# A decode attention layer on one core: whole-tile VectorE steps, a re-tiled query projection, and a wo block in small transfers

## The chip, the core and the metric

The kernel runs on one core of a Trainium2 chip. The core has a matrix engine (TensorE, "PE"; its weight loads are "PEld"), VectorE ("DVE"), ScalarE ("ACT"), GpSimd ("POOL") and SyncE ("SP"), which here only issues transfers. Sixteen DMA engines move data from the device memory into the on-chip memory of 128 partitions. Each engine runs its own list of instructions in order; engines wait for each other on semaphores.

The metric is the device time of one execution in microseconds. Before the change it is 664.11 us, the median of three runs (664.04 to 664.16).

## The reference, cut to what matters

Four requests, one new token each. The token's vector of 640 numbers is normalised; from it a query projection gives 32 heads of 128 numbers, and each head attends over its own cache of 4096 keys and values. The result goes through `wo`. A small gated MLP on the same normalised vector and the token itself are added.

```python
x = A_x                                   # (4, 1, 640)
xn = _layernorm(x)
q = (xn @ wq).reshape(B, 1, 32, 128).transpose(0, 2, 1, 3)
scores = jnp.einsum('bhqd,bhkd->bhqk', q, k_cache) * 128 ** -0.5    # k_cache (4, 32, 4096, 128)
p = softmax(scores)
o = jnp.einsum('bhqk,bhkd->bhqd', p, v_cache)
A = o.transpose(0, 2, 1, 3).reshape(B, 1, 4096) @ wo                # wo (4096, 640)
out = x + A + gated_mlp(xn, w_in, w_sp, b_sp, w_out)
```

Everything is bfloat16. The caches are 2 x 134 MB and each element is used once, so nearly all bytes that are read are keys and values.

## The kernel before

**Tiles and slots.** The 32 heads are cut into 8 groups (`HG`) of 4 heads (`HT`). A tile is one group of one request: 4 heads x 4096 positions x 128, 4 MB, laid over 128 partitions so that partition 32h + l holds 128 consecutive positions (`NC` "columns" of 128 numbers) of head h; the 32 partitions of a head are its "lanes" (`LN`). There are 32 tiles of keys and 32 of values; tile i is group i // 4, request i % 4. All of them pass through five slots of 4 MB (`KV_SLOTS`), which at the start hold the two parts of `wq` and the MLP's weights.

**Loads.** All large loads are issued by SyncE. `loads` (L128) is the order: keys 0 and 1, then values i and keys i + 2 in turn, with one more key tile ahead before tiles 24 and 28 (`EXTRA_K`). `pump` (L140) issues the next loads whose slots are marked as used; SyncE then waits until the engines have really finished with the slot. The last values are cut in four. The blocks of `wo` (640 KB, one for each group) are loaded by `load_wo` (L153): blocks 0 to 6 at the end of the third tile of their group (L698), block 7 at the end in four parts (L157).

**Start.** x is normalised and transposed to `xnT`. The query projection (L267 to L276) has the weights of `wq` as the stationary operand, 128 x 128 for each of 32 heads and 5 slices of the 640 inputs, and 4 columns of `xnT` moving: 160 matmuls; the result, `qT`, has the head's 128 numbers along the partitions. `stage_q` (L421) makes of it, tile by tile, a query for each of the 128 lanes: a transpose once a group, then one matmul with `q_lanes`, copied to `qbc` by ScalarE. `gmlp` computes the MLP. GpSimd prepares constants.

**The loop over tiles** (L662 to L699) is written out by hand: inside `manual_schedule` TensorE, VectorE, ScalarE and SyncE keep the order of the code. For tile i:

- Keys: VectorE multiplies the tile in place by the query (`product`, L441), folds 128 numbers to 64 by one addition (`fold_half`, L450), TensorE adds the 64 in steps of 8 through the identity (`sums`, L459, eight matmuls of 512 columns), and VectorE sums the last 8 (`row_sums`, L470). All of this is done in two halves of 64 columns, `product(i, 0)`, `fold_half(i, 0)`, `sums(i, 0)`, then the same for half 1; `row_sums(i, 1)` comes in tile i + 1, after `product(i + 1, 0)`.
- Softmax of tile i - 1, spread over tile i: the lanes' maximum (`lane_max`, L479, VectorE), laid out by ScalarE (L485), spread to the head by a matmul (L492), the head's maximum `nb` (`head_max`, L499, VectorE, after the first fold of tile i), the exponentials (`exps`, L508, ScalarE), and the mask on GpSimd (L517), which lays p out for the value matmuls as `pm`.
- Values of tile j = i - 1 (i - 2 and i - 3 after the extra key tiles): `blocks` (L532), 32 matmuls on 32 columns each, four side by side; for odd j a copy (L542) and `gather` (L553).
- At a group's last tile: denominators (`group_den`, L577 to L586: GpSimd, TensorE, VectorE's reciprocal), `group_norm` (L591), `group_turn`, and one tile later `group_pick` and `group_proj` (L631), eight matmuls of the group's result with its `wo` block into `out_ps`.

On TensorE the order in a tile is therefore: spread of the maximum, `sums` of half 0, the query, the value blocks of tile j, gather, `sums` of half 1. On VectorE it is: product 0, row sums 1 of the last tile, lane maximum, fold 0, head maximum, product 1, (reciprocal), row sums 0, fold 1, (group norm).

**End.** After the loop come the softmax of tile 31, the last two value tiles, the group's norm, `group_proj` of group 7, copies of `out_ps` and the transfers of the output.

Of the kernel before, what the change touches and what calls it, by code (L numbers as in the profile page):

```python
# [15 lines left out]
KV_SLOTS = 5  # L16
EXTRA_K = (24, 28)
ALIGN = 512


@with_exitstack
def kernel(
# [130 lines left out]
    def load_wo(j):  # L153
        wo_tiles[j] = wop.tile([P, HT, D], BF16, name="wo")
        if j == HG - 1:
            for hh in range(HT):
                nc.sync.dma_start(out=wo_tiles[j][:, hh, :], in_=wo_h[j][:, hh, :])  # L157
            return
        nc.sync.dma_start(out=wo_tiles[j][:].rearrange("p r n -> p (r n)"), in_=wo_r[j])

    pump()

# [100 lines left out]
    xnT = const.tile([P, DC, Bsz], BF16)  # L263
    nc.vector.tensor_copy(out=xnT[:], in_=xnT_ps[:])

    q_ps = ps_m.tile([P, H, Bsz], FP32, tag="m", name="q_ps")
    for h in range(H):  # L267
        for c in range(DC):
            t, i = wq_parts[c]
# [38 lines left out]
    def gmlp():  # L308
        zz, gw, gt, gz, sq = (gm[n] for n in ("zz", "gw", "gt", "gz", "sq"))
        zT = ps_pv.tile([P, 2, NFC, Bsz], FP32, tag="pv", name="zT")  # L310
        for t in range(2):
            f1 = t * Fh + NFF * P
            w_t = w_in_sb[:, :, t * Fh : f1].rearrange("p c (f k) -> p c k f", k=NFF)
            for k in range(NFC):
                for c in range(DC):
                    nc.tensor.matmul(
                        out=zT[: P if k < NFF else FT, t, k, :],
                        lhsT=w_t[:, c, k, :] if k < NFF else w_in_sb[:, c, f1 : f1 + FT],
                        rhs=xnT[:, c, :],
                        start=(c == 0),  # L320
                        stop=(c == DC - 1),
                    )
# [93 lines left out]
    qbcs, scores, pvs, blocks_sb = {}, {}, {}, {}  # L416
    sums_ps, maxes = {}, {}

    q_rows = {}

    def stage_q(i):  # L421
        hg, b = divmod(i, Bsz)
        if b == 0:
            qr_ps = ps_m.tile([HT * Bsz, Dh], BF16, tag="m", name="qr_ps")
            nc.tensor.transpose(
                out=qr_ps[:],
                in_=qT[:, HT * hg : HT * (hg + 1), :].rearrange("p h b -> p (h b)"),
                identity=ident[:],
            )
            q_rows[hg] = small.tile([HT * Bsz, Dh], BF16, name="q_rows")  # L430
            nc.scalar.copy(out=q_rows[hg][:], in_=qr_ps[:])  # L431
        qb_ps = ps_m.tile([P, Dh], FP32, tag="m", name="qbc_ps")
        nc.tensor.matmul(  # L433
            out=qb_ps[:], lhsT=q_lanes[:, b, :], rhs=q_rows[hg][:], start=True, stop=True
        )
        qbcs[i] = small.tile([P, Dh], BF16, name="qbc", bufs=3)
        nc.scalar.copy(out=qbcs[i][:], in_=qb_ps[:])  # L437

    def product(i, half):
        t = k_tiles[i][:, half * HC : (half + 1) * HC, :]  # L440
        nc.vector.tensor_tensor(  # L441
            out=t,
            in0=t,
            in1=qbcs[i][:, None, :].to_broadcast([P, HC, Dh]),
            op=ALU.mult,
        )

    def fold_half(i, half):
        t = k_tiles[i][:, half * HC : (half + 1) * HC, :]
        nc.vector.tensor_tensor(  # L450
            out=t[:, :, 0:HD2], in0=t[:, :, 0:HD2], in1=t[:, :, HD2:Dh], op=ALU.add
        )

    def sums(i, half):
        t = k_tiles[i][:, half * HC : (half + 1) * HC, :]
        s = sums_ps[i, half] = ps_s.tile([P, HC, RW], FP32, name="s_ps")
        n = HD2 // RW
        for g in range(n):
            nc.tensor.matmul(  # L459
                out=s[:],  # L460
                lhsT=ident[:],
                rhs=t[:, :, g * RW : (g + 1) * RW],
                start=(g == 0),
                stop=(g == n - 1),
            )

    def row_sums(i, half):
        if half == 0:
            scores[i] = small.tile([P, NC], FP32, name="s_sb")
        nc.vector.tensor_reduce(  # L470
            out=scores[i][:, half * HC : (half + 1) * HC],
            in_=sums_ps.pop((i, half))[:],
            axis=AX.X,
            op=ALU.add,
        )

    def lane_max(i):
# [165 lines left out]
    def at(i, fn, *args):  # L643
        if 0 <= i < NT:
            fn(i, *args)
# [9 lines left out]
    E = mybir.EngineType  # L655
    with tc.manual_schedule(engines={E.PE, E.DVE, E.Activation, E.SP}):
        stage_q(0)
        stage_q(1)
# [94 lines left out]
```

## Time and profile before

| | |
|---|---|
| median of 3 runs | 664.11 us (664.04 to 664.16) |
| the profiled execution: its time / its span | 664.67 us / 662.8 us |
| busy: TensorE, VectorE, ScalarE, GpSimd | 52%, 74%, 8%, 23% of the span |
| read from device memory | 282.24 MB, 426 GB/s over the span |
| products (L441): number, mean | 64, 4.42 us |
| folds (L450): number, mean | 64, 2.37 us |
| GpSimd masks (L517): number, mean | 32, 4.45 us |
| VectorE idle before products, waiting for keys | 100.2 us |

The profile is of one execution; times in it are microseconds from the start of the span. A line of a group reads: source line, engine, operation, tile written <- tiles read, shape, number; in a timeline the two numbers in front are start and duration, and in brackets stands how long the engine was idle before and what ended that. In the chain of waits each row is start, duration and what the time went to; "DMA x<-y" is a transfer from its issue to its landing. An engine's name with a q (SPq) is its sequencer, which issues transfers. In the list of DMA queues q1 is SyncE's, q10 ScalarE's, and q8 and q14 read program code; the columns are packets, MB and share of the sixteen engines' time.

### The profile page before, as it was taken

How to read it: one execution, taken by the hardware profiler on the slowest of the kernel's cores; microseconds unless marked ns; L12 is line 12 of the kernel's file. 1: busy time of each engine (PE TensorE's matmuls, PEld its weight loads, DVE VectorE, ACT ScalarE, POOL GpSimd, SP SyncE). 2: the span in 40 equal slices, each digit the busy share in tenths (PEclk: the TensorE clock that was granted, in tenths of full speed). 3: DMA queues.
4: the chain of work that ended last, by engine and by line, in shares of the span. 5: the costliest groups of instructions: out<-in, count | busy, mean ns of one | idle time of the engine just before them, and what ended most of it. 6: DMA issues, size and time to landing. Idle time of an engine off the chain costs nothing.

```text
span 662.8 us, 5338 instructions
## 1 busy us (share of the span) xinstructions
PE 344.5 (52%) x2205; PEld 144.1 (22%) x2205; DVE 492.9 (74%) x334; ACT 52.5 (8%) x161; POOL 150.2 (23%) x51
## 2 busy tenths in 40 slices
PE   0636553636646545653437644474654655434576
PEld 0512221212222121221212212131211212212133
DVE  3289797867789677788767698767787899776960
ACT  0201100000010000100000001000100000000010
POOL 2002222112222112222112222112222132222220
PEclk9998676777576677776776657758666767678676
DMA  8999999999999999999999999999999999999996
GB/s 368 430 438 423 434 439 432 431 437 422 436 429 436 437 424 437 432 430 437 431 429 437 424 439 435 428 439 428 431 439 427 432 436 426 439 424 437 437 422 262
DMA packets 11972, 282.59 MB, mean 426 GB/s; under 512 B 1344, under 2 KB 1964, under 8 KB 3244
## 3 DMA queue, kind: packets, MB, share of 16 engines
q1 hardware_dynamic: 11928, 282.25, 99.0%
q8 instruction: 17, 0.28, 0.2%
q14 instruction: 7, 0.06, 0.0%
q10 hardware_dynamic: 20, 0.01, 0.0%
HBM read 282.24 MB, written 0.01 MB: 426 GB/s over the span
## 4 chain that ended last, share of the span: by engine, by line
issue 44%; DMA 29%; POOL 14%; DVE 9%; PE 3%; SPq 0%; ACT 0%; POOLq 0%; DVEq 0%; ACTq 0%
DMA k_nat<-in_A_k_cache_dram 21%; POOL pm L517 14%; DMA v_nat<-in_A_v_cache_dram 6%; DVE k_nat L441 5%; DVE k_nat L450 3%; PE s_ps L459 2%; DMA wo<-in_A_wo_dram 2%; PE pv_acc L532 1%; DVE s_sb L470 1%; DVE m L479 0%; PE pv L553 0%; POOL own_sum L577 0%; SPq L92 0%; SPq L104 0%; ACT pv_sb L542 0%
## 5 line engine op out<-in xcount | busy, mean ns | idle before, releaser
L441 DVE TENSOR_TENSOR k_nat<-k_nat,qbc 128x8192 bf16<-128x8192 bf16 x64 | 282.9, 4420 | 100.4 <-DMA k_nat<-in_A_k_cache_dram 100.2
L517 POOL TENSOR_TENSOR pm<-p,hmask_bf 128x512 bf16<-128x512 bf16 x32 | 142.4, 4452 | 496.2 <-ACT p L508 496.2
L459 PE MATMUL s_ps<-k_nat,ident 128*128 128x512 bf16 x512 | 188.9, 535 | 67.0 <-DVE k_nat L450 67.0
L450 DVE TENSOR_TENSOR k_nat<-k_nat 128x4096 bf16<-128x4096 bf16 x64 | 151.9, 2373 | 0.0
L492 PE MATMUL max_ps<-lay,head_scale 128*128 128x32 f32 x64 | 19.0, 388 | 176.3 <-ACT lay L485 176.3
L532 PE MATMUL pv_acc<-v_nat,pm 128*32 128x512 bf16 x1008 | 85.0, 498 | 39.0 <-POOL pm L517 35.6
L459 PEld LDWEIGHTS <-ident 128*128 128x128 bf16 x512 | 67.6, 134 | 168.6 <-issue 151.1
L492 PEld LDWEIGHTS max_ps<-lay,head_scale 128*128 128x128 f32 x64 | 14.8, 288 | 190.5 <-ACT lay L485 190.5
L532 PEld LDWEIGHTS <-pm 128*32 128x32 bf16 x1008 | 29.5, 117 | 82.4 <-POOL pm L517 42.1
L470 DVE TENSOR_REDUCE s_sb<-s_ps 128x64 f32<-128x512 f32 x64 | 43.4, 677 | 4.1 <-PE s_ps L459 4.1
L485 ACT ACTIVATE lay<-lane_diag,m 128x32 f32<-128x32 f32 x32 | 10.3, 321 | 340.2 <-DVE m L479 340.2
L586 DVE RECIPROCAL rden<-den 128x16 f32<-128x16 f32 x8 | 2.1, 258 | 30.5 <-PE den L584 30.5
L553 PE MATMUL pv<-sel,pv_sb 128*128 128x8 f32 x128 | 18.6, 272 | 9.3 <-ACT pv_sb L542 9.3
L553 PEld LDWEIGHTS pv<-sel,pv_sb 128*128 128x128 f32 x128 | 17.1, 208 | 15.8 <-ACT pv_sb L542 15.8
L508 ACT ACTIVATE p<-s_sb,nb 128x128 bf16<-128x128 f32 x32 | 12.8, 401 | 63.8 <-DVE nb L499 63.8
L437 ACT CAST qbc<-qbc_ps 128x128 bf16<-128x128 f32 x32 | 8.4, 267 | 85.1 <-PE qbc_ps L433 85.1
L542 ACT COPY pv_sb<-pv_acc 128x512 f32<-128x512 f32 x16 | 9.4, 586 | 65.6 <-PE pv_acc L532 65.6
L479 DVE TENSOR_REDUCE m<-s_sb 128x1 f32<-128x128 f32 x32 | 9.2, 286 | 1.1
L433 PE MATMUL qbc_ps<-q_rows,q_lanes 16*128 16x128 bf16 x32 | 8.2, 264 | 2.7 <-ACT q_rows L431 2.7
L278 DVE CAST qT<-q_ps 128x128 bf16<-128x128 f32 x1 | 0.3, 292 | 12.5 <-PE q_ps L270 12.5
L270 PE MATMUL q_ps<-xnT,wq 128*128 128x4 bf16 x160 | 4.6, 166 | 8.7 <-DMA wq<-in_A_wq_dram 8.7
L631 PE MATMUL out_ps<-wo,o_r 128*4 128x320 bf16 x56 | 8.0, 435 | 0.0
(90 smaller groups left out, 89.7 us busy)
## 6 DMA issues: line engine op xcount, KB each, us to landing
k_nat<-in_A_k_cache_dram SPq DMA_DIRECT2D x32, 4096.0 KB, 38.7
v_nat<-in_A_v_cache_dram SPq DMA_DIRECT2D x31, 4096.0 KB, 33.3
wo<-in_A_wo_dram SPq DMA_DIRECT2D x7, 640.0 KB, 40.5
wq<-in_A_wq_dram SPq DMA_DIRECT2D x1, 4096.0 KB, 12.7
w_sb<-in_B_w_in_dram SPq DMA_DIRECT2D x1, 2160.0 KB, 19.4
v_nat<-in_A_v_cache_dram SPq DMA_DIRECT2D x1, 2048.0 KB
wq<-in_A_wq_dram SPq DMA_DIRECT2D x1, 1024.0 KB, 14.7
v_nat<-in_A_v_cache_dram SPq DMA_DIRECT2D x1, 1024.0 KB
```

What stands on the lines that cost most here:

```text
L441: nc.vector.tensor_tensor(out=t, in0=t, in1=qbcs[i][:, None, :].to_broadcast([P, HC, Dh]), op=ALU.mult,)
L450: nc.vector.tensor_tensor(out=t[:, :, 0:HD2], in0=t[:, :, 0:HD2], in1=t[:, :, HD2:Dh], op=ALU.add)
L459: nc.tensor.matmul(out=s[:], lhsT=ident[:], rhs=t[:, :, g * RW : (g + 1) * RW], start=(g == 0), stop=(g == n - 1),)
L470: nc.vector.tensor_reduce(out=scores[i][:, half * HC : (half + 1) * HC], in_=sums_ps.pop((i, half))[:], axis=AX.X, op=ALU.add,)
L479: nc.vector.tensor_reduce(out=m1[:], in_=scores[i][:], axis=AX.X, op=ALU.max)
L485: nc.scalar.activation(out=d[:], in_=lane_diag[:], func=ACT.Copy, scale=maxes[i][:, 0:1])
L492: nc.tensor.matmul(out=ps[:], lhsT=head_scale[:], rhs=maxes[i][:], start=True, stop=True)
L508: nc.scalar.activation(out=p[:], in_=scores.pop(i)[:], func=ACT.Exp, bias=nb[:], scale=scale_qk, accum_out=acc[hg % NACC][:, b : b + 1],)
L517: nc.gpsimd.tensor_tensor(out=p_m[b][:, :, e : e + GC * HT].rearrange("p g (c h) -> p g c h", h=HT), in0=p[:].rearrange("p (g c) -> p g c" ...
L532: nc.tensor.matmul(out=pv_acc[g * LN : (g + 1) * LN, :], lhsT=pm[:, c // GC, :], rhs=v_nat[:, c : c + GC, :].rearrange("p c d -> p (c d)") ...
L542: nc.scalar.copy(out=pv_sb[:], in_=pv_acc[:])
L553: nc.tensor.matmul(out=pvs[hg][:, :, b - 1 : b + 1], lhsT=pv_sb[:, k * Dh : (k + 1) * Dh], rhs=sel[:, k, :, :], start=(k == 0), stop=stop ...
```

## The change

- **VectorE's steps are a whole tile each.** `product(i)`, `fold(i)` and `row_sums(i)` work on 128 columns at once; `sums(i)` is 16 matmuls into one buffer of two banks (`ps_s` has one buffer instead of two). The order in a tile becomes, on VectorE: product, row sums of the last tile, lane maximum, fold, head maximum, (reciprocal, group norm); on TensorE: spread of the maximum, (queries of the next group), value blocks of tile j, gather, all of `sums(i)`.
- **The query projection** has `xnT` (padded with zeros to 32 columns) as the stationary operand and 512 columns of `wq` moving: 5 slices x 8 groups, 40 matmuls, each group on its own 32 output partitions. VectorE and ScalarE copy one half of the result each. `stage_q` now works a group at a time: four matmuls with a new constant `place` gather the group's heads, then four with `q_lanes` make the queries of all four requests; it is called once before the loop and in the third tile of each group.
- **wo block 6** is loaded after the loop, ahead of block 7, and `group_proj(6)` is called just before `group_proj(7)`. The pool of `wo` tiles has two buffers.
- **wo block 0** is loaded in nine transfers: eight of 8 partitions each, then one of the other 64.

```diff
+WO_PARTS = (*range(0, 65, 8), 128)
...
-    wop = ctx.enter_context(tc.tile_pool(name="wop", bufs=1))
+    wop = ctx.enter_context(tc.tile_pool(name="wop", bufs=2))
...
-    ps_s = ctx.enter_context(tc.tile_pool(name="ps_s", bufs=2, space=PSUM))
+    ps_s = ctx.enter_context(tc.tile_pool(name="ps_s", bufs=1, space=PSUM))
...
-        nc.sync.dma_start(out=wo_tiles[j][:].rearrange("p r n -> p (r n)"), in_=wo_r[j])
+        rows = wo_tiles[j][:].rearrange("p r n -> p (r n)")
+        parts = WO_PARTS if j == 0 else (0, P)
+        for p0, p1 in zip(parts, parts[1:]):
+            nc.sync.dma_start(out=rows[p0:p1], in_=wo_r[j][p0:p1])
...
+    place = const.tile([P, HT, HT * Bsz], BF16)
+    nc.gpsimd.memset(place[:], 0.0)
+    for hh in range(HT):
+        nc.gpsimd.tensor_copy(
+            out=place[:, hh, hh * Bsz : (hh + 1) * Bsz], in_=lane_diag[:, 0:Bsz]
+        )
...
+    xnT = const.tile([P, DC, LN], BF16)
+    nc.gpsimd.memset(xnT[:], 0.0)
+    nc.vector.tensor_copy(out=xnT[:, :, 0:Bsz], in_=xnT_ps[:])
+
+    q_sb = const.tile([P, HG // CG, HT * Dh], BF16)
...
+    for c in range(DC):
+        t, i = wq_parts[c]
+        for hg in range(HG):
+            g = hg % CG
             nc.tensor.matmul(
-                out=q_ps[:, h, :],
-                lhsT=t[:, i, h * Dh : (h + 1) * Dh],
-                rhs=xnT[:, c, :],
+                out=q_ps[hg // CG][g * LN : (g + 1) * LN, :],
+                lhsT=xnT[:, c, :],
+                rhs=t[:, i, hg * HT * Dh : (hg + 1) * HT * Dh],
                 start=(c == 0),
                 stop=(c == DC - 1),
             )
-    qT = const.tile([P, H, Bsz], BF16)
-    nc.vector.tensor_copy(out=qT[:], in_=q_ps[:])
+    nc.vector.tensor_copy(out=q_sb[:, 0, :], in_=q_ps[0][:])
+    nc.scalar.copy(out=q_sb[:, 1, :], in_=q_ps[1][:])
...
-    def stage_q(i):
...
+    def stage_q(hg):
+        g, ps = hg % CG, slice(hg % CG * LN, (hg % CG + 1) * LN)
+        qr_ps = ps_m.tile([HT * Bsz, Dh], FP32, tag="m", name="qr_ps")
+        for hh in range(HT):
+            nc.tensor.matmul(
...
+                lhsT=place[ps, hh, :],
+                rhs=q_sb[ps, hg // CG, hh * Dh : (hh + 1) * Dh],
...
+        qb_ps = ps_m.tile([P, Bsz, Dh], FP32, tag="m", name="qbc_ps")
+        for b in range(Bsz):
+            nc.tensor.matmul(
+                out=qb_ps[:, b, :], lhsT=q_lanes[:, b, :], rhs=q_rows[:], start=True, stop=True
+            )
...
         for i in range(NT):
             j = turns.get(i)
-            product(i, 0)
-            at(i - 1, row_sums, 1)
+            product(i)
+            at(i - 1, row_sums)
             at(i - 1, lane_max)
             at(i - 1, lay_max)
             at(i - 1, spread_max)
             group(turns.get(i - 1, -1), group_pick)
-            group(turns.get(i - 1, -1), group_proj)
-            fold_half(i, 0)
+            if turns.get(i - 1, -1) // Bsz < HG - 2:
+                group(turns.get(i - 1, -1), group_proj)
+            fold(i)
             at(i - 1, head_max)
             at(i - 1, exps)
-            sums(i, 0)
-            product(i, 1)
-            if i + 2 < NT:
-                stage_q(i + 2)
+            if i % Bsz == 2 and i // Bsz + 1 < HG:
+                stage_q(i // Bsz + 1)
...
-            row_sums(i, 0)
-            fold_half(i, 1)
             if due:
                 gather(due[-1])
             for jj in due:
                 group(jj, group_norm)
-            sums(i, 1)
+            sums(i)
...
-            if i % Bsz == 2 and i // Bsz < HG - 1:
+            if i % Bsz == 2 and i // Bsz < HG - 2:
                 load_wo(i // Bsz)
+        load_wo(HG - 2)
         load_wo(HG - 1)
-        row_sums(NT - 1, 1)
+        row_sums(NT - 1)
...
         group_norm(HG - 1)
+        group_proj(HG - 2)
         group_proj(HG - 1)
```

More of the change, by code (lines that the diff above doesn't have):

```diff
@@ L262 @@
         )
[L263 to L269, printed above, removed]
+    xnT = const.tile([P, DC, LN], BF16)
+    nc.gpsimd.memset(xnT[:], 0.0)
+    nc.vector.tensor_copy(out=xnT[:, :, 0:Bsz], in_=xnT_ps[:])
+    q_sb = const.tile([P, HG // CG, HT * Dh], BF16)
+    q_ps = [
+        ps_m.tile([P, HT * Dh], FP32, tag="m", name="q_ps") for _ in range(HG // CG)
+    ]
+    for c in range(DC):
+        t, i = wq_parts[c]
+        for hg in range(HG):
+            g = hg % CG
             nc.tensor.matmul(
-                out=q_ps[:, h, :],
-                lhsT=t[:, i, h * Dh : (h + 1) * Dh],
-                rhs=xnT[:, c, :],
+                out=q_ps[hg // CG][g * LN : (g + 1) * LN, :],
+                lhsT=xnT[:, c, :],
+                rhs=t[:, i, hg * HT * Dh : (hg + 1) * HT * Dh],
                 start=(c == 0),
@@ L318, in gmlp @@
                         lhsT=w_t[:, c, k, :] if k < NFF else w_in_sb[:, c, f1 : f1 + FT],
-                        rhs=xnT[:, c, :],
+                        rhs=xnT[:, c, 0:Bsz],
                         start=(c == 0),
@@ L417, with product @@
     sums_ps, maxes = {}, {}
-    q_rows = {}
-    def stage_q(i):
[L422 to L425, printed above, removed]
+    def stage_q(hg):
[3 more added lines that the diff above has]
+            nc.tensor.matmul(
                 out=qr_ps[:],
-                in_=qT[:, HT * hg : HT * (hg + 1), :].rearrange("p h b -> p (h b)"),
-                identity=ident[:],
-            )
[L430 to L440, printed above, removed]
+                lhsT=place[ps, hh, :],
+                rhs=q_sb[ps, hg // CG, hh * Dh : (hh + 1) * Dh],
+                start=(hh == 0),
+                stop=(hh == HT - 1),
+            )
+        q_rows = small.tile([HT * Bsz, Dh], BF16, name="q_rows")
+        nc.scalar.copy(out=q_rows[:], in_=qr_ps[:])
+        qb_ps = ps_m.tile([P, Bsz, Dh], FP32, tag="m", name="qbc_ps")
[3 more added lines that the diff above has]
+            )
+        qbcs[hg] = small.tile([P, Bsz, Dh], BF16, name="qbc")
+        nc.scalar.copy(out=qbcs[hg][:], in_=qb_ps[:])
+    def product(i):
+        t = k_tiles[i]
         nc.vector.tensor_tensor(
@@ L443, in product, with fold @@
             in0=t,
-            in1=qbcs[i][:, None, :].to_broadcast([P, HC, Dh]),
+            in1=qbcs[i // Bsz][:, i % Bsz, None, :].to_broadcast([P, NC, Dh]),
             op=ALU.mult,
         )
-    def fold_half(i, half):
-        t = k_tiles[i][:, half * HC : (half + 1) * HC, :]
+    def fold(i):
+        t = k_tiles[i]
         nc.vector.tensor_tensor(
@@ L452, in fold_half, with sums, row_sums @@
         )
-    def sums(i, half):
-        t = k_tiles[i][:, half * HC : (half + 1) * HC, :]
-        s = sums_ps[i, half] = ps_s.tile([P, HC, RW], FP32, name="s_ps")
+    def sums(i):
+        s = sums_ps[i] = ps_s.tile([P, NC, RW], FP32, name="s_ps")
         n = HD2 // RW
[L458 to L469, printed above, removed]
+        for half in range(2):
+            cs = slice(half * HC, (half + 1) * HC)
+            for g in range(n):
+                nc.tensor.matmul(
+                    out=s[:, cs, :],
+                    lhsT=ident[:],
+                    rhs=k_tiles[i][:, cs, g * RW : (g + 1) * RW],
+                    start=(g == 0),
+                    stop=(g == n - 1),
+                )
+    def row_sums(i):
+        scores[i] = small.tile([P, NC], FP32, name="s_sb")
         nc.vector.tensor_reduce(
[L471 to L474, printed above, removed]
+            out=scores[i][:], in_=sums_ps.pop(i)[:], axis=AX.X, op=ALU.add
         )
@@ L657 @@
         stage_q(0)
-        stage_q(1)
         gmlp()
```

## The prediction

> **What bounds the kernel now.** I read the page first, then the end of the chain of waits, then SyncE's issues and waits, then a timeline of one tile.
>
> ```profile
> span 662.8 us, 5338 instructions
> DMA  8999999999999999999999999999999999999996
> q1 hardware_dynamic: 11928, 282.25, 99.0%
> q8 instruction: 17, 0.28, 0.2%
> ...
> q10 hardware_dynamic: 20, 0.01, 0.0%
> ```
>
> The sixteen DMA engines are busy for 99% of the span while VectorE, the busiest engine, has 74%. One 4 MB tile takes 9.67 us; no slice between the first and the last falls below nine tenths. So a change pays only where it feeds, balances or ends the stream. The chain of waits ends on it:
>
> ```profile
> 606.26 40.90 DMA v_nat<-in_A_v_cache_dram
> 647.16 0.02 issue
> 647.17 12.45 DMA wo<-in_A_wo_dram
> 659.62 0.04 issue
> 659.66 0.47 PE out_ps L631 x2
> ```
>
> The last wo part lands at 659.62; 3.16 us later the span is over. The trace keeps sixteen landing events for each transfer. For the part before that one they run from 655.00 to 658.23: seven DMA engines within 1.0 us of the first, nine 2.5 to 3.2 us behind. The lag is made by q8's reads of program code, 16 KB each: after the read at 66.3 one landing of the sixteen goes from 0.2 to 1.7 us behind, after those at 114.7 and 154.3 another. The read at 657.6 delays one engine of the last part by 1 us more.
>
> ```profile
> 80.40 0.33 SPq L123 DMA_DIRECT2D v_nat<-in_A_v_cache_dram  x1
> 83.88 0.33 SPq L123 DMA_DIRECT2D k_nat<-in_A_k_cache_dram  x1
> 84.26 0.43 SPq L159 DMA_DIRECT2D wo<-in_A_wo_dram  x1
> 98.04 0.33 SPq L123 DMA_DIRECT2D v_nat<-in_A_v_cache_dram  x1
> ```
>
> ```profile
> SPq L157 <- DMA v_nat<-in_A_v_cache_dram: 16.5, 2, 9.3
> SPq L123 <- DMA wq<-in_A_wq_dram: 9.4, 1, 9.4
> ```
>
> SyncE issues tiles 30 to 43 us before they land. The two waits are the ones to see: k tile 1 is issued at 13.46, when the first wq transfer, eight transfers back, lands at 13.45; the last two wo parts go out at 637.49 and 647.17, when the transfers eight back land (637.48 and 647.16). The completion counts rotate over eight: a transfer is issued only after the eighth before it has landed.
>
> ```profile
> 150.26 0.18 DVE L499 TENSOR_REDUCE nb<-max_ps 128x1 f32<-128x32 f32 x1
> 150.36 4.42 DVE L441 TENSOR_TENSOR k_nat<-k_nat,qbc 128x8192 bf16<-128x8192 bf16 x1
> 151.11 4.56 POOL L517 TENSOR_TENSOR pm<-p,hmask_bf 128x512 bf16<-128x512 bf16 x1 [15.96 <-ACT p L508]
> 154.70 0.68 DVE L470 TENSOR_REDUCE s_sb<-s_ps 128x64 f32<-128x512 f32 x1
> 155.30 2.53 DVE L450 TENSOR_TENSOR k_nat<-k_nat 128x4096 bf16<-128x4096 bf16 x1
> ...
> 645.81 1.04 POOL L517 TENSOR_TENSOR pm<-p,hmask_bf 128x512 bf16<-128x512 bf16 x1 [9.04 <-ACT p L508]
> ```
>
> GpSimd's mask takes 1.04 us with VectorE idle, but 4.56 when it starts 0.75 us after a product: it ends 0.9 us after the product does. It stands still while a product runs. Where it is first, VectorE waits: the fold at 155.30 takes 2.53 instead of 2.28.
>
> **The change, part by part.** VectorE's steps whole. From the two shapes (8192 elements 4.42 us, 4096 2.28) one fixed part is 0.15 us; whole, a product is 8.69, a fold 4.41, row sums 1.21. Against two halves that is 0.15 less for each, 0.45 a tile, on an engine that waits 100 us for keys: nothing. What counts is the order. A tile's keys landing at T: product to T+8.6, the last tile's row sums and maximum 1.45, fold 4.33, nb at T+14.4; the mask starts 0.85 after nb's start (150.26 to 151.11), at T+15.2, and the next keys land at T+19.4. VectorE is idle between, so the mask takes 1.04: T+16.3. TensorE's value blocks take 3.5 (T+19.8), for odd tiles the copy and gather 1.6 more, then sixteen sums at 1.9 for eight: T+23.6 or T+25.2. Before, these sums ended some 19 to 21 us after T. The keys' buffer comes free 4 us later, the values' about 3, and the queue had 16 us or more in hand at each k and v issue (issue to the landing of the transfer ahead): covered. At a group's end VectorE waits for the denominators and the gather (the product starts 2.3 us late); a wo block stretches the following gap to 20.9, and the mask still starts 2.9 us ahead of the product.
>
> That cover has a cliff. If a product starts before the mask, the mask waits 8.7 us; the value blocks, the sums queued behind them on TensorE, and VectorE's row sums come later, the next keys have landed, and the next mask is again behind a product. It is priced below. The closest place is the start: keys 0 land at 34.77; products 8.73 and 8.61, folds 4.34 and 4.33, row sums and maximum 1.45, then 0.87 put the first mask at 63.12; keys 2 land at 63.74. The margin is 0.6 us, and since both ends follow the same slowest DMA engine, three tiles apart, it moves little.
>
> [...]
>
> The query projection. 160 matmuls with 128-column weights (4.6 us busy) become 40 of the 128*32 form, of which 32 take 3.49 in the value blocks: 4.4 us, the first 32 already when the first wq part lands (13.45). It ends near 18 instead of 20.2; the two copies (0.6) run on two engines. GpSimd's place tile and memset fit before 13.4. Staging a group's four queries at once adds matmuls of 0.1 to 0.2 us ahead of the value blocks, where TensorE waits for the mask. All this lies before keys 0 land at 34.77, or in waits: nothing. TensorE's instructions fall by 240 and rise by 48, of 4410; at one code read per 256 there are 16 reads, and the one at 657.6 leaves the end (my estimate: the last near 649).
>
> The wo block 0 in nine transfers. SyncE gets them after the issue of keys 5, at about 89. By the rotation over eight, the seventh waits for values 3 (112.1), the eighth for keys 5 (last landing 121.75), the ninth for the first part. Values 4 and keys 6, issued at 98.0 and 100.1 before, are queued on SyncE behind them. So the DMA engines run dry: eighth part at 121.78, ninth at 122.20 (0.42 an issue, the wo row), first packet 0.95 later (0.75 to 1.02 in the first and last transfers), its four rows an engine at 0.196: values 4 start at 123.9 on every engine. Before, engines started them at 121.29 (leading) to 123.29. The leading ones lose 2.6, the laggards 0.6, and the old lag is wiped out. From there the leading engines take as long as before (655.42 minus 121.29: 534.1), to 658.1; thirteen code reads remain, on the nine engines seen lagging, so some get two at 1.5: 661.1. Against 659.62 that is +1.5.
>
> Bounds: if SyncE isn't held, +0, or below: how the parts spread over engines is not in the trace for 8 lanes, but ACT's queue, q10, shows 20 packets for transfers of 4, 1, 1 and 4 rows, a row and a count each, so few rows use few engines. Were the eight leading engines given 12 rows and the others 4, the laggards gain 4 times 0.19. Upwards, one more code read on a late engine adds 1.5. I take +1.5, by the wait's rows.
>
> [...]
>
> The later wo block 6. Same bytes, issued behind the last values, so these land 1.5 us earlier relative to the stream's end. Two buffers: no wait. But its projection now waits for it at the end: it lands 1.7 us before the last part (four parts at 0.42), then sixteen matmuls at 1.23 for eight: 0.8 us after the last landing where two matmuls took 0.5. +0.3. [...]
>
> Sum: 0 + 0 + 1.5 + 0.3 = +1.8 on the profiled execution's own 664.67 (span 662.8 and 1.9 around it), 666.5; that run stands 0.56 above the median, so 665.9.
>
> **Rivals.** (a) The stall is covered or absent and the parts only balance. For: seven leading engines. Against: the waits at 13.45, 637.48 and 647.16. The laggards end 0.76 earlier, without the code read (1.0) and with +0.3 of the tail: 664.1 minus 1.4, 662.7, not slower. It decides if values 4 are issued before 121.3. (b) The cliff: a mask behind a product, at the start. Then a tile takes 5.9 (row sums to nb) + 8.7 + 0.9 + 3.5 + 3.8 = 22.8, odd 24.4, a group's end 21.9, a group of four 92 against the stream's 79. It holds until the values lag by two tiles (tile 25): six groups, 80 us, less at most 16 in hand: 64 to 80, some 735. It decides when the first mask starts after 63.74. For: a margin of 0.6 of a 28 us chain. Against: every step in it is a row. (c) The stall costs only what the laggards lose (0.6) and the tail is hidden: 664.7, no change.
>
> **How the numbers follow.** Forecast 0.50 (665 to 668), (c) 0.17, (a) 0.18, (b) 0.15. About 0.2% (1.3 us) is what tells a difference from none: the forecast gives slower 0.45 and same 0.05; (c) same; (a) faster 0.11, same 0.07; (b) slower. Faster 0.11, same 0.29, slower 0.60. The range 662.4 to 668.2 leaves out (b) and little else.
>
> **What would show it.** GpSimd's mask 1.04 us in nearly all tiles (4.45 now) and its busy time a third; VectorE still waiting for keys; SyncE's values 4 at about 122.6 and a dip of the DMA rate near 122; the last landing near 661. Wrong if a mask takes 8 to 9 us, if the values 4 go out near 100, or if code reads fall on other engines.

## The result, and the profile after

The change makes the kernel slower: 668.35 us (median of ten; 667.66 to 674.43) against 664.17 us before, a ratio of 1.0068 (95% interval 1.0053 to 1.0084), 4.2 us. The forecast had the sign right, but it was 665.9, a loss of 1.8, and its range ended at 668.2. One thing is needed to read the numbers below: of the executions of kernels with the new query projection (the one that falls off the cliff aside) 9 of 83 took 3.6 to 6.1 us more than the median of their kernel, and none of 89 without it; the three of them that were profiled (one transfer, two of 64 lanes, block 6 in the loop) show the 32 KB packets between 20 and 64 us at a median of 1.36 us instead of 1.21, so from these three profiles only durations and distances are taken, and why it happens stays open.

The profiled execution took 668.47 us, its span is 666.7. From its page (first the span, then the DMA engines' busy share and the rate in forty slices of 16.7 us, then two queues):

```profile
span 666.7 us, 5055 instructions
...
DMA  9999999899999999999999999999999999999996
GB/s 373 423 438 437 432 423 435 317 425 439 440 429 426 440 430 427 427 444 427 434 436 429 432 436 437 426 432 438 427 432 436 431 430 436 432 436 427 432 428 278
...
q1 hardware_dynamic: 11992, 282.25, 98.7%
q8 instruction: 16, 0.26, 0.1%
```

The same bytes move, and the eighth slice, 116.7 to 133.3 us, is the only one between the first and the last that falls out of the row: 317 GB/s. It lacks some 115 GB/s over 16.7 us, 1.9 MB, which at the usual 432 GB/s is 4.4 us. So the whole loss lies in one place. q8 has one read of program code fewer, as forecast.

SyncE's timeline around that place:

```profile
83.72 0.33 SPq L124 DMA_DIRECT2D v_nat<-in_A_v_cache_dram  x1
88.93 0.33 SPq L124 DMA_DIRECT2D k_nat<-in_A_k_cache_dram  x1
89.31 34.01 SPq L163 DMA_DIRECT2D wo<-in_A_wo_dram  x9
123.41 0.53 SPq L124 DMA_DIRECT2D v_nat<-in_A_v_cache_dram  x1
124.05 0.36 SPq L124 DMA_DIRECT2D k_nat<-in_A_k_cache_dram  x1
```

Its waits:

```profile
SPq L163 <- DMA k_nat<-in_A_k_cache_dram: 19.5, 2, 10.1
SPq L163 <- DMA v_nat<-in_A_v_cache_dram: 11.3, 2, 9.4
```

The nine transfers of wo block 0 take SyncE 34 us to issue, and 30.8 of these it waits for key and value tiles to land: the rotation over eight. Parts five to eight go out at 92.66, 102.37, 112.03 and 122.44, each just after the transfer eight back has landed. I call this the hold. The values 4 go out at 123.41; before the change they went out at 98.04.

Windows of the kernel after (start:end, length, busy time of each engine, TensorE's clock, and last the DMA engines' share and the rate in GB/s):

```profile
118.00:120.00 2.00, 1.21 (x12) 0.46 (x16) 0.00 (x0) 0.00 (x0) 0.91 (x2) 0.50 0.85 341
120.00:122.00 2.00, 2.00 (x24) 0.64 (x16) 0.00 (x0) 0.00 (x0) 0.00 (x0) 0.50 0.40 109
122.00:124.00 2.00, 1.80 (x10) 1.37 (x7) 0.26 (x1) 0.58 (x1) 0.00 (x0) 0.50 0.07 26
124.00:126.00 2.00, 2.00 (x8) 1.27 (x9) 0.95 (x2) 0.00 (x0) 0.00 (x0) 0.50 1.56 426
126.00:128.00 2.00, 2.00 (x7) 0.71 (x6) 2.00 (x1) 0.00 (x0) 0.00 (x0) 0.57 0.61 262
```

The second and third of these in the kernel before:

```profile
120.00:122.00 2.00, 1.21 (x4) 0.44 (x4) 0.98 (x3) 0.00 (x0) 0.00 (x0) 0.82 1.04 437
122.00:124.00 2.00, 2.00 (x9) 0.81 (x7) 2.00 (x1) 0.00 (x0) 0.00 (x0) 0.50 1.21 520
```

For four microseconds the stream is nearly dry (109 and 26 GB/s, where it was 437 and 520).

VectorE and GpSimd at the first mask, two timelines of the kernel after:

```profile
57.82 4.41 DVE L470 TENSOR_TENSOR k_nat<-k_nat 128x8192 bf16<-128x8192 bf16 x1
62.15 0.18 DVE L516 TENSOR_REDUCE nb<-max_ps 128x1 f32<-128x32 f32 x1
63.68 8.92 DVE L461 TENSOR_TENSOR k_nat<-k_nat,qbc 128x16384 bf16<-128x16384 bf16 x1 [1.34 <-DMA k_nat<-in_A_k_cache_dram]
```

```profile
63.01 1.04 POOL L534 TENSOR_TENSOR pm<-p,hmask_bf 128x512 bf16<-128x512 bf16 x1 [54.87 <-ACT p L525]
79.16 1.04 POOL L534 TENSOR_TENSOR pm<-p,hmask_bf 128x512 bf16<-128x512 bf16 x1 [15.11 <-ACT q_rows L450]
```

The mask starts 0.67 us ahead of product 2, and GpSimd is busy 63.4 us in the whole span (150.2 before). That part of the change does what it says.

The end of the chain of waits:

```profile
633.48 28.18 DMA wo<-in_A_wo_dram
661.70 2.34 PE out_ps L648 x16
```

The two projections stand back to back, sixteen matmuls. The last transfer, behind the one in the chain, has its last landing at 663.33; before, the last landing was at 659.62.

### The profile page after: what moved, and what is told of

Same layout as the page of the kernel before. It is cut to its first block, busy times and chain, and to the rows that moved or that the text cites. A ratio compares the mean times of both kernels' runs of the same rounds, so it can differ in the third digit from the quotient of the medians.

```text
span 666.7 us, 5055 instructions
## 1 busy us (share of the span) xinstructions
PE 318.8 (48%) x2109; PEld 144.2 (22%) x2109; DVE 480.3 (72%) x238; ACT 48.4 (7%) x138; POOL 63.4 (10%) x57
## 4 chain that ended last, share of the span: by engine, by line
issue 63%; DMA 18%; DVE 9%; PE 5%; POOL 4%; SPq 1%; ACT 0%; POOLq 0%; ACTq 0%; DVEq 0%
DMA k_nat<-in_A_k_cache_dram 14%; DVE k_nat L461 4%; DMA wo<-in_A_wo_dram 4%; POOL pm L534 3%; PE s_ps L480 3%; DVE k_nat L470 3%; PE pv_acc L549 1%; DVE s_sb L490 1%; PE pv L570 0%; PE out_ps L648 0%; SPq L124 0%; ACT p L525 0%; DVE m L496 0%; ACT pv_sb L559 0%; POOL own_sum L594 0%
## 5 line engine op out<-in xcount | busy, mean ns | idle before, releaser
L461 DVE TENSOR_TENSOR k_nat<-k_nat,qbc 128x16384 bf16<-128x16384 bf16 x32 | 278.3, 8696 | 92.7 <-DMA k_nat<-in_A_k_cache_dram 92.7
L549 PE MATMUL pv_acc<-v_nat,pm 128*32 128x512 bf16 x1008 | 106.2, 597 | 91.6 <-POOL pm L534 90.8
L480 PE MATMUL s_ps<-k_nat,ident 128*128 128x512 bf16 x512 | 139.2, 434 | 21.2 <-DVE k_nat L470 21.2
L470 DVE TENSOR_TENSOR k_nat<-k_nat 128x8192 bf16<-128x8192 bf16 x32 | 141.3, 4415 | 0.0
L534 POOL TENSOR_TENSOR pm<-p,hmask_bf 128x512 bf16<-128x512 bf16 x32 | 56.6, 1769 | 587.8 <-ACT p L525 572.7
L480 PEld LDWEIGHTS <-ident 128*128 128x128 bf16 x512 | 55.0, 112 | 103.9 <-issue 54.3
L549 PEld LDWEIGHTS <-pm 128*32 128x32 bf16 x1008 | 33.7, 136 | 146.8 <-POOL pm L534 97.2
L490 DVE TENSOR_REDUCE s_sb<-s_ps 128x128 f32<-128x1024 f32 x32 | 39.0, 1217 | 9.6 <-PE s_ps L480 9.6
L453 PE MATMUL qbc_ps<-q_rows,q_lanes 16*128 16x128 bf16 x32 | 4.4, 284 | 25.9 <-ACT q_rows L450 25.9
L289 PE MATMUL q_ps<-wq,xnT 128*32 128x512 bf16 x40 | 4.5, 629 | 8.3 <-DMA wq<-in_A_wq_dram 8.3
```

The source lines that it names most:

```text
L461: nc.vector.tensor_tensor(out=t, in0=t, in1=qbcs[i // Bsz][:, i % Bsz, None, :].to_broadcast([P, NC, Dh]), op=ALU.mult,)
L470: nc.vector.tensor_tensor(out=t[:, :, 0:HD2], in0=t[:, :, 0:HD2], in1=t[:, :, HD2:Dh], op=ALU.add)
L480: nc.tensor.matmul(out=s[:, cs, :], lhsT=ident[:], rhs=k_tiles[i][:, cs, g * RW : (g + 1) * RW], start=(g == 0), stop=(g == n - 1),)
L490: nc.vector.tensor_reduce(out=scores[i][:], in_=sums_ps.pop(i)[:], axis=AX.X, op=ALU.add)
L534: nc.gpsimd.tensor_tensor(out=p_m[b][:, :, e : e + GC * HT].rearrange("p g (c h) -> p g c h", h=HT), in0=p[:].rearrange("p (g c) -> p g c" ...
L549: nc.tensor.matmul(out=pv_acc[g * LN : (g + 1) * LN, :], lhsT=pm[:, c // GC, :], rhs=v_nat[:, c : c + GC, :].rearrange("p c d -> p (c d)") ...
```

## The experiments

Unless a line says otherwise each kernel is the kernel after with only the lines shown changed, and times are medians beside runs of the kernel before on the same chip (664.4 to 664.5 us).

### One transfer, six, seven; and the whole steps alone

```diff
-WO_PARTS = (*range(0, 65, 8), 128)
+WO_PARTS = (0, 128)
```

> The kernel after, with wo block 0 in one transfer again instead of nine; all else as after. Theory A (the nine transfers hold SyncE until keys 5 have landed, and the restart of the stream costs the late DMA engines about 3.4 us and the leading ones 5): the values 4 are issued near 98 instead of 123.4, the dip in the DMA rate near 122 is gone, and the time falls by 3.5 to 5 us, to 663.4 to 665. Rival B (the whole-tile VectorE steps, the query projection or the later wo block 6 cost the time, the stall is covered): it stays within 1 us of after, 667.4 to 669.4. In between (665 to 667.4) both have a part.

Measured: 663.65 us; ratio to the kernel before 0.9995 (0.9984 to 1.0006). The nine transfers carry the whole loss, 4.7 us. What is left of the change is a little below the kernel before or level with it.

```diff
+WO_PARTS = (0, 8, 16, 24, 32, 64, 128)
```

> The kernel after, with wo block 0 in six transfers: four of 8 lanes, one of 32, one of 64. Theory A: with six, the sixth waits for keys 4, which have landed near 102, and the values 4 behind them for values 3 (landing near 112): they go out before the stream is empty, so nothing stalls and the time is that of one transfer, 663 to 665. If it is the small descriptors of 8 lanes that cost and not the wait, about half of the loss stays, 665.5 to 667.

Measured: 666.96 us; ratio 1.0045 (1.0032 to 1.0058). My theory A misses: nothing holds the values 4 (issued at 112.16, twelve microseconds before the last wo row starts), and still 3.3 of the 4.7 us are lost. The windows of this run:

```profile
118.00:120.00 2.00, 1.16 (x12) 0.46 (x16) 0.00 (x0) 0.00 (x0) 0.96 (x2) 0.50 0.93 363
120.00:122.00 2.00, 2.00 (x25) 0.66 (x17) 0.00 (x0) 0.00 (x0) 0.00 (x0) 0.62 1.18 236
122.00:124.00 2.00, 1.58 (x16) 1.36 (x13) 0.37 (x2) 0.58 (x1) 0.00 (x0) 1.00 1.18 247
124.00:126.00 2.00, 2.00 (x11) 0.90 (x10) 1.99 (x2) 0.00 (x0) 0.00 (x0) 1.00 0.81 269
126.00:128.00 2.00, 1.41 (x11) 0.64 (x8) 2.00 (x1) 0.00 (x0) 0.00 (x0) 1.00 0.99 426
```

Here the DMA engines are busy all the time (a share of about 1) and yet move 236 to 269 GB/s. That is not a stall; the packets themselves are slow. A packet of keys or values is 32 KB, a packet of `wo` is one row of 5 KB, for one of the 128 lanes (partitions). The trace's packets by the microsecond in which they start (number, mean duration, shortest and longest):

```
119  32 KB  4x 1.78 [1.28-2.23]   5 KB 20x 0.20 [0.20-0.20]
120  32 KB  2x 2.54 [2.54-2.54]   5 KB 33x 0.42 [0.28-0.60]
121  32 KB  3x 2.71 [2.54-2.80]   5 KB 27x 0.38 [0.35-0.58]
122  32 KB  3x 2.53 [2.50-2.55]   5 KB 25x 0.41 [0.37-0.49]
123  32 KB  6x 2.22 [2.02-2.59]   5 KB 14x 0.45 [0.39-0.52]
124  32 KB  6x 1.73 [1.60-1.91]   5 KB  9x 0.39 [0.33-0.61]
125  32 KB  9x 1.31 [1.22-1.57]
126  32 KB 13x 1.22 [1.21-1.22]
```

Both kinds take about twice their time, the key and value packets beside the wo rows as well. In the kernel before, with one transfer, all of them stay at 0.20 and 1.21 in the same microseconds. I had not thought of this, and the next experiments had to find what makes them slow.

Seven transfers, the last 64 lanes cut into two of 32:

```diff
+WO_PARTS = (0, 8, 16, 24, 32, 64, 96, 128)
```

> [...] Theory A: by the rotation over eight the values 4 are now the eighth transfer behind keys 5 and are issued only when these have landed, near 122, so the DMA engines stand still but for the rows of the last parts: slower than six transfers by 2.5 to 4.5 us, 666 to 668.5. If the number of transfers has a smooth price, the step from six to seven is under 1 us.

Measured: 668.17 us; ratio 1.0069 (1.0049 to 1.0089). The values 4 are issued at 123.83 as said, behind the landing of keys 5, so the rotation is right to the transfer. But the step from six to seven costs 1.2 us, not 2.5 to 4.5: most of the loss is there without the hold.

The kernel before, with VectorE's steps whole and nothing else:

```diff
-            product(i, 0)
+            product(i)
...
-            fold_half(i, 0)
+            fold(i)
...
-            sums(i, 0)
-            product(i, 1)
...
+            sums(i)
```

> The kernel before, with VectorE's steps a whole tile each and nothing else of the change. Theory A: the DMA stream sets the time and the steps are covered: 664.2 plus or minus 0.6, GpSimd's mask near 1.04 us in nearly all tiles. Rival B: the whole steps alone carry a part of the loss, 665.5 to 668. Rival C: the first mask falls behind a product without the new query projection, some 64 to 80 us more.

Measured: 664.67 us; ratio 1.0005 (0.9996 to 1.0013). The group of GpSimd's masks in this run (busy, mean ns):

```profile
L514 POOL TENSOR_TENSOR pm<-p,hmask_bf 128x512 bf16<-128x512 bf16 x32 | 56.6, 1768 | 586.5 <-ACT p L505 513.5
```

A mask falls from 4.45 to 1.77 us and the time does not move: GpSimd was off the path, as the prediction had it.

### What makes the packets slow, and what the hold costs

Three kernels with block 0 cut in other ways, all else as with one transfer. First by lanes:

```diff
+WO_PARTS = (0, 64, 128)
```

> The kernel with one transfer, but wo block 0 in two transfers of 64 neighbouring lanes. Nothing holds SyncE. In the trace of six transfers the rows of 5120 bytes took 0.38 to 0.45 us instead of 0.20 and the 32 KB packets beside them up to 2.8 instead of 1.21, for some 5 us. Theory L (transfers that fill only lanes 0 to 63, or only 64 to 127, run at half rate, whatever their number): rows near 0.39 us again, eight of them an engine 3.1 us instead of 1.6, so 1.2 to 2.2 us above one transfer (663.65): 664.9 to 665.9. Theory N (the number of transfers costs, about 0.6 us each as from one to six): 664.0 to 664.4, rows at 0.20.

Measured: 667.4 us; ratio 1.0053 (1.0037 to 1.007). Two transfers are enough: 3.7 us above one (3.4 without the execution of 671.02), more than I expected. The 5 KB rows take 0.37 to 0.39 us in the mean from 124 to 127 us, the 32 KB packets 2.0 to 2.6 until 129. I had counted the rows, but not the value tile's packets beside and just behind them. The window in the middle of the rows:

```profile
124.00:126.00 2.00, 2.00 (x24) 0.65 (x16) 0.00 (x0) 0.00 (x0) 0.00 (x0) 0.50 1.05 221
```

Then by columns:

```diff
+WO_CUTS = (0, 1280, 2560)
...
-        for p0, p1 in zip(parts, parts[1:]):
-            nc.sync.dma_start(out=rows[p0:p1], in_=wo_r[j][p0:p1])
+        for c0, c1 in zip(cuts, cuts[1:]):
+            nc.sync.dma_start(out=rows[:, c0:c1], in_=wo_r[j][:, c0:c1])
```

> The same bytes in two transfers as well, but each of all 128 lanes and half of the columns (rows of 2560 bytes). Theory L: no row is slowed (0.10 us each) and the time is that of one transfer, 663.3 to 664.1. Theory N: as the two transfers of 64 lanes, 664.0 to 664.4, and not below that kernel.

Measured: 663.77 us; ratio 0.9991 (0.9983 to 1.0000). The same bytes, the same number of transfers, all 128 lanes in each: nothing is lost, and the 32 KB packets stay at 1.21. The window of the rows in this run:

```profile
120.00:122.00 2.00, 2.00 (x24) 0.65 (x16) 0.00 (x0) 0.00 (x0) 0.00 (x0) 0.54 1.10 456
```

So it is not the number of transfers; it is which lanes one transfer fills.

Then nine transfers by columns, which hold SyncE as the kernel after does:

```diff
+WO_CUTS = (*range(0, 2273, 284), 2560)
```

> Nine transfers as in the kernel after, so SyncE is held as there (the values 4 issued near 122.5), but each of all 128 lanes and a ninth of the columns: the hold without the narrow transfers. By the sum of the prediction the hold makes every DMA engine start the values 4 at 123.9, and two program reads of 1.5 us later the last landing is 661.1, 2.5 us later than one transfer without hold: 665.5 to 666.7. If the hold costs all that nine transfers cost: 667.6 to 668.6. If the narrow transfers alone cost it: 663.3 to 664.3.

Measured: 666.84 us; ratio 1.0038 (1.0025 to 1.0051): 3.1 us above two transfers by columns, for the hold alone. (Its 1152 short rows take 2.3 us of each DMA engine instead of 1.6, but eight of the nine parts are brought while the stream is dry.) SyncE issues the values 4 at 122.51. The windows:

```profile
118.00:120.00 2.00, 1.36 (x16) 0.55 (x20) 0.00 (x0) 0.00 (x0) 0.76 (x2) 0.50 0.95 385
120.00:122.00 2.00, 2.00 (x24) 0.53 (x16) 0.00 (x0) 0.00 (x0) 0.00 (x0) 0.50 0.63 194
122.00:124.00 2.00, 1.79 (x15) 1.51 (x12) 0.26 (x1) 0.58 (x1) 0.00 (x0) 0.81 1.29 339
124.00:126.00 2.00, 2.00 (x11) 0.88 (x10) 1.91 (x2) 0.00 (x0) 0.00 (x0) 1.00 0.66 279
126.00:128.00 2.00, 1.60 (x12) 0.74 (x9) 2.00 (x1) 0.00 (x0) 0.00 (x0) 1.00 0.88 377
```

The share falls with the rate in the window from 120 to 122 (0.63 and 194): this is a stream that runs dry. When it starts again, the first sixteen 32 KB packets take 1.57 to 2.07 us, mean 1.88, and the next ones 1.22. The last landing is at 661.63, and in the run with two transfers by columns at 658.58; the difference, 3.05, is that of the two times. The prediction's own sum for the hold gave a last landing of 661.1, 0.5 us less; it has no term for the 0.7 us that the first packets lose.

The two causes do not add up to the kernel after. The hold alone costs 3.1, the six transfers 3.3, both together 4.7: in the kernel after the 56 rows of the first seven parts are brought between 119 and 122.5 us, while the stream is running dry anyway.

### Can the early DMA engines take over rows?

Block 3 in sixteen transfers of eight lanes, every fourth lane of 32, spread over five tiles so that the stream does not run dry:

```diff
+LANES = {10: (0, 3), 11: (3, 6), 12: (6, 9), 13: (9, 12), 14: (12, 16)}
...
+        for n in range(n0, n1):
+            p0 = n // 4 * 32 + n % 4
+            ps = slice(p0, p0 + 29, 4)
+            nc.sync.dma_start(out=rows[ps], in_=wo_r[j][ps])
```

> Block 0 in one transfer; wo block 3 in sixteen transfers of eight lanes, every fourth lane of 32, three a tile in tiles 10 to 14, so that nothing holds SyncE. Eight landing events each: eight DMA engines move the whole block, 16 rows of 0.196 us each, the other eight none. If the leading engines are these eight and each engine's own work sets its end, the late ones have 8 rows less: 1.3 to 1.6 us below one transfer, 662.0 to 662.4. If the late engines are these eight: 1.6 us above, 665.2. If what is behind the half rate is that a group of lanes takes only so many bytes a microsecond, whichever engine brings them, nothing is gained: 663.4 to 664.6, with rows of half of the transfers near 0.39. [...]

Measured: 668.36 us; ratio 1.007 (1.0051 to 1.009), 4.7 above one transfer, far outside all three expectations. The windows in which rows of the first, second, fourth and fifth batch land:

```profile
276.00:280.00 4.00, 3.16 (x32) 1.12 (x32) 0.00 (x0) 0.00 (x0) 0.96 (x2) 0.50 0.97 412
...
296.00:300.00 4.00, 0.86 (x12) 0.34 (x16) 1.38 (x2) 0.49 (x2) 1.04 (x1) 0.50 1.01 432
...
340.00:344.00 4.00, 4.00 (x24) 1.42 (x17) 1.80 (x1) 0.00 (x0) 0.00 (x0) 0.77 0.98 343
...
360.00:364.00 4.00, 3.68 (x34) 1.90 (x24) 0.28 (x2) 0.58 (x1) 0.00 (x0) 0.71 1.01 270
```

The DMA share is 1 in all four; the rate is not. The first two batches fill lanes below 64: their rows, at 277 to 281 and 299 to 300 us, take 0.20 us, and the 32 KB packets stay at 1.21. The last two fill lanes from 64 on, by transfers of the same shape and with as many landings: rows of 0.28 and 0.31 us in the mean, and 32 KB packets at a mean of 1.79 (those that start from 340 to 342) and 2.09 (360 to 362). In the third batch one of three parts is for lanes above, and the 32 KB packets that start from 320 to 321 take 1.37. So transfers to eight lanes below 64 run at full speed; with rows for the lanes above the packets beside them slow down.

Why the lanes from 64 on differ was not shown: the trace gives the time and the size of a packet, neither its engine nor its lanes.

This run also tells whether the eight engines lead or trail. Landing events, as offsets in us: the sixteen of wo block 2 from 279.35, the transfer just ahead of the parts, and the eight of the first part, from 279.55:

```
16: 0.00 0.01 0.02 0.05 0.17 0.23 0.26 0.55 0.93 0.94 1.35 1.36 1.56 1.64 1.73 1.91
 8: 0.00 0.01 0.18 0.27 0.56 0.95 1.36 1.65
```

Each of the eight is 0.20 us, one row, behind an event of the sixteen: four of them lead (up to 0.27 us), one stands in the middle, three trail by 0.95 or more. Moving rows to these engines takes work from late ones and gives it to other late ones. In the end the sixteen landings of the last wo part lie 6.2 us apart (3.3 in the run with two transfers by columns). How the 4.7 us divide between this and the slow packets was not tried.

### The cliff, and the late wo block

Two kernels with one more VectorE instruction ahead of product 1, on a tile of its own; all else as with one transfer:

```diff
+            if i == 1:
+                nc.vector.tensor_tensor(
+                    out=late[:], in0=late[:], in1=late[:], op=ALU.mult
+                )
             product(i)
```

> The kernel with one transfer, and one more VectorE product of 384 numbers a partition on a tile of its own, ahead of product 1 (0.15 fixed and 0.2 us by the products' rows: 0.35 us). The first mask then starts near 63.4, still ahead of product 2, which starts when keys 2 land at 63.7. By rival (b) of the prediction nothing happens below the margin of 0.66: 663.2 to 664.1, masks 1.04 us.

Measured: 663.62 us. The added product took 0.35 us, the first mask started at 63.22, product 2 at 63.61, and the second mask took 1.04 us like the first.

> The same with 2048 numbers (0.15 and 1.05, 1.2 us): the first mask would start at 64.2, after product 2. By rival (b) it stands still behind the product, 8.7 us, and every later one too, until the values lag by two tiles: masks of 8 to 9.7 us, GpSimd busy above 150 us, and 64 to 80 us more: 728 to 744. If the order recovers by itself after a tile or two: under 10 us more, 664 to 674, with a few long masks.

Measured: 756.35 us, the median of four executions: three took 755.35 to 759.19, one 668.12. The added product took 1.22 us. The profile is of the one of 759.19. VectorE and then GpSimd in this run, timelines:

```profile
63.26 0.18 DVE L519 TENSOR_REDUCE nb<-max_ps 128x1 f32<-128x32 f32 x1
63.65 8.69 DVE L464 TENSOR_TENSOR k_nat<-k_nat,qbc 128x16384 bf16<-128x16384 bf16 x1 [0.21 <-DMA k_nat<-in_A_k_cache_dram]
81.01 1.23 DVE L493 TENSOR_REDUCE s_sb<-s_ps 128x128 f32<-128x1024 f32 x1 [8.66 <-PE s_ps L483]
```

```profile
64.12 9.12 POOL L537 TENSOR_TENSOR pm<-p,hmask_bf 128x512 bf16<-128x512 bf16 x1 [55.08 <-ACT p L528]
87.66 8.82 POOL L537 TENSOR_TENSOR pm<-p,hmask_bf 128x512 bf16<-128x512 bf16 x1 [14.42 <-ACT q_rows L453]
114.22 8.83 POOL L537 TENSOR_TENSOR pm<-p,hmask_bf 128x512 bf16<-128x512 bf16 x1 [17.73 <-ACT p L528]
138.15 1.04 POOL L537 TENSOR_TENSOR pm<-p,hmask_bf 128x512 bf16<-128x512 bf16 x1 [15.10 <-ACT p L528]
```

Product 2 starts at 63.65, the mask 0.47 us later, and it stands still until the product ends. VectorE then waits 8.66 us for the sums, the next keys have landed, and the next mask is behind a product again. Only at a group's end, where VectorE waits for the denominators, does a mask get through; the pattern, three long and one short, holds to 617.77, and 23 of the 32 masks are long. Rival (b) is real, and the change stands 0.67 us in front of it. Its price is 92 to 96 us in these three executions rather than the 64 to 80 that I had worked out: a group of four takes some 96 us (short mask to short mask: 138.15, 234.67, 330.31) against the 92 of the sum, and it does not end at tile 25.

The execution of 668.12 was not profiled, so what spared it is not shown. The profile of one transfer gives a hint: there keys 2 land late, the first mask starts at 64.04 and product 2 only at 67.92, and 1.2 us more would not use up that margin of 3.88.

With wo block 6 loaded and projected in the loop again:

```diff
-            if turns.get(i - 1, -1) // Bsz < HG - 2:
-                group(turns.get(i - 1, -1), group_proj)
+            group(turns.get(i - 1, -1), group_proj)
...
-        load_wo(HG - 2)
...
-        group_proj(HG - 2)
```

> The kernel with one transfer, and wo block 6 loaded and projected in the loop as before the change: whole-tile steps and the new query projection are left of it. By the sum the tail after the last landing is 0.5 us instead of 0.75, and the last program read is at 650 to 654 instead of 655.5 to 657.6: 0.2 to 0.3 below one transfer, 663.3 to 663.5, and 0.8 to 1.1 below the kernel before. If the place of wo block 6 is what brings the 0.7 against before, it is lost: 664.2 to 664.7.

Measured: 663.93 us; ratio to before 1.0002 (0.9986 to 1.0019), so neither of the two can be told from one transfer's 663.65. The end of its chain:

```profile
658.81 1.88 PE pv L570 x8
660.69 1.71 PE pv L582 x64
662.66 1.27 PE out_ps L648 x8
```

The gain of 0.3 was an error of mine: the last landing is at 662.70, and the eight matmuls of block 7 end 1.23 us after it, because TensorE is still at the values when the first wo parts land. With block 6 between the last values and block 7, TensorE is ahead, and the tail is 0.7 us.

Last, the nine transfers alone, in the kernel before:

```diff
+WO_PARTS = (*range(0, 65, 8), 128)
...
-        nc.sync.dma_start(out=wo_tiles[j][:].rearrange("p r n -> p (r n)"), in_=wo_r[j])
+        for p0, p1 in zip(parts, parts[1:]):
+            nc.sync.dma_start(out=rows[p0:p1], in_=wo_r[j][p0:p1])
```

> The kernel before, with wo block 0 in the nine transfers and nothing else of the change. If their price does not depend on the other parts it is 668.35 minus 663.65, 4.7 us: 668.6 to 669.6. If VectorE's half steps, which end a tile's keys earlier, take up a part of the stall: 666 to 668. Nothing: 664.4.

Measured: 668.62 us; ratio 1.0063 (1.0051 to 1.0075), 4.1 above the kernel before. They bring the loss by themselves, with half steps as with whole ones.

## Why the prediction was right and wrong

- **Whole steps, "nothing": right.** Alone they are at 1.0005 of before. The durations came out as worked out (8.70, 4.42 and 1.22 us against 8.69, 4.41 and 1.21), and GpSimd's masks take 1.04 us in 29 of 32 tiles (8.83 in the other three).
- **Query projection, "nothing" and one program read fewer: right** in the count (16: from the first read to the last one comes every 255 instructions of TensorE in the mean, and every 254 before) and in that the typical time does not move with it; that 9 of 83 executions with it take some 4 us more had no term in the sum. The last read came at 655.5, not near 649, but in the run shown no landing of the last part stands apart, as one did before by 1.0 us. In the run with two transfers by columns the last landing is at 658.58, against 659.62 before: the same 1.0 us, which the prediction puts down to the read at 657.6; no run tried that alone. This and the tail leave what is below the kernel before, 0.6 us, less than a measurement can tell.
- **The hold on SyncE: right in its mechanism and its place.** Parts seven and eight waited for values 3 and keys 5; the ninth followed the eighth after 0.05 us, with no wait of its own. The values 4 went out at 123.41 (122.6 said), and the old lag was wiped out.
- **Its price, "+1.5": the step that failed.** It reads: the last part's first packet 0.95 after its issue at 122.20, "its four rows an engine at 0.196: values 4 start at 123.9 on every engine", and from there as before. In the trace the last packets of keys 5, beside the first narrow rows, take 1.34 to 1.87 us, keys 5 land at 122.42 instead of 121.75, and the last part is issued at 122.76. Its rows start at 124.1; the first sixteen take 0.26 to 0.89 us, the other 48 a mean of 0.24. The values 4 start at 125.1 to 125.95, and their first packets take 1.81 instead of 1.21 us. That is 1.2 to 2.0 us of start and 0.6 of first packets, and the last landing is at 663.33 instead of 661.1. Two things were missing from the sum: in the transfers that filled only a part of the lanes rows were slower and slowed the packets beside them (two transfers of 64 lanes: rows at 0.37 to 0.39 us, 3.7 us without any hold), and the first packets after a standstill were slow (1.88 us, where the hold was tried alone). The run with the hold alone divides the 2.2 us: its last landing, 661.63, is 0.5 above the sum's, and the narrow transfers make the other 1.7. I had priced a row by the row of a 128-lane transfer.
- **Tail, "+0.3": 0.7 after the last landing, as said to a tenth**, but the 0.5 it was compared with belonged to a last landing that stood 1.0 us behind the others.
- **Rival (a), the parts balance the engines: wrong.** The values 4 went out after 121.3, and where the hold is absent sixteen eight-lane transfers of block 3 cost 4.7 us. The bound that I worked out for it, 0.76 us for the late engines, rested on the eight engines of a part being the leading ones; by the landings of block 3's first part they are a mixture (four lead, one stands in the middle, three trail).
- **Rival (b), the cliff: did not happen, and exists** on the side of the margin that was named; its price was too low by 12 us or more. That the margin "moves little" does not hold in every execution: it is 0.67 us in the kernel after and 3.88 in the profile of one transfer.
- **Rival (c), 0.6 for the late engines: wrong.** It took the rows at full speed as well.

## What to carry to other kernels

Cut a transfer by columns, not by lanes: here two column halves cost nothing and two halves of the lanes 3.7 us, and the slow rows had slow packets beside them. Count how many issues stand between a large transfer and the next on its queue; here an issue waits until the eighth transfer before it has landed (the eighth part went out at 122.44, the last landing of keys 5 was at 122.42), and a stream that stops once costs its wait and slow first packets besides (a mean of 1.81 and 1.88 us instead of 1.21). Price a packet by a row of the same lanes and the same neighbours, and where a change has a cliff, measure the distance to it by a small known delay on either side.

## What the runs showed of the hardware

- A DMA engine that reads as busy is not one that moves bytes: a share of 1.18 went with 236 GB/s where 437 is usual.
- Of batches of eight-lane transfers of one shape, those into lanes below 64 ran at full speed (rows 0.20 us, 32 KB packets 1.21), and those into lanes from 64 on slowed the 32 KB packets beside them to means of 1.79 and 2.09 us, some to 2.2.
- After the standstill the first sixteen 32 KB packets took 1.6 to 2.1 us instead of 1.21, in the kernel after and in the hold tried alone. Why was not tried.
- One GpSimd mask of 1.04 us that came 0.47 us too late was followed by 22 more that stood behind a product, and the kernel took 92 to 96 us more in three of four executions; where it came 0.39 us early nothing was lost.
